# Attention decode with a side MLP on one core: K and V of a block through three rotating slots, each block finished before the next is scored

## The chip, the cores and the metric

The kernel runs on one core of one Trainium2 chip. The metric is the device time of one execution in microseconds, the median of the runs shown. Times inside the execution come from one profiled execution and count from the start of its span.

## What is computed

One token, `D = 1024`, goes through two branches that are added to it. Branch A is attention with 32 query heads on 4 key/value heads, over a cache of 65536 keys of 128 numbers. Branch B is a small MLP with two gelu stages. All tensors are bfloat16.

```python
xn = layernorm(x)
# A: 4 KV heads, 8 query heads on each, 65536 keys
q = xn @ wq                                   # 1024 x 4096
p = softmax((q . k_cache) * 128 ** -0.5)      # per head, over all keys
A = (p . v_cache) @ wo                        # 4096 x 1024
# B: h is shifted by quarters of its columns (S = 1: only zeros or the row itself)
h  = gelu(layernorm(xn) @ w1);  x1 = xn + shift(h) @ w2
B  = x1 + gelu(layernorm(x1) @ w3) @ w4       # 1024 x 3584, 3584 x 1024
out = x + A + B
```

With one row every shifted quarter is zero, so `x1` is `xn`. The kernel still reads `w1` and `w2`.

Nearly all the work is reading: 134.2 MB of cache (4 heads x 65536 keys x 128 x 2 bytes, for K and for V) and the rest weights, 169.87 MB in all.

## The kernel before, in words

**Blocks.** The cache of each KV head is cut into `NB = 2` blocks of 32768 keys. So there are `NU = 8` blocks `u`, and block `u` belongs to head group `g = u // 2`. K of a block, or V of a block, is one transfer of 128 partitions x 32768 bfloat16, 8.39 MB (`load`, L291 to L312). The weights come in similar pieces: `wq` and `wo` 8.39 MB each, `w3` 7.34 MB, `w12` (that is w1 and w2 in two transfers) 4.19 MB, `w4` 7.34 MB in five transfers.

**Slots.** SBUF holds three slots of that size (`slots`). `home` (L285 to L288) says which item lies where: K of even blocks in slot 0, K of odd blocks in slot 2, V of all blocks in slot 1 (the last V in slot 0). `wq`, `w3` and `w12` start in slots 0, 1 and 2, `wo` and `w4` end in 1 and 2.

**Recorded program.** The kernel does not issue its instructions at once. It records them in program order (`Program.add`); `plan` works out which semaphore each must wait for from the regions it reads and writes, and `emit` writes them out, each engine's in the recorded order. So the order of the calls in the source is the order on each engine, and an instruction that waits holds up all that stands behind it on its engine. Since all operations are emitted by the same helper lines, the profile shows few lines: L82 is every recorded DVE, ACT and POOL operation, L102 the weight loads, L106 the matmuls of `mm`, L116 `mm32`, L122 `turn32`, L89 the transfers. One reads it by tiles: `slot` (the three slots), `sc` (scores in PSUM), `p_sb` (the weights after the exponential), `oacc` (P·V in PSUM), `psB` (the final projection).

**Transfers.** All large loads stand on the queue of SP, in recorded order. A load into a slot waits until TensorE has read the last of what lay there.

**One block** passes through four steps:

- `scores(u)` (L453): DVE transposes K of the block in place, in 4 pieces (`slot<-slot`, 128x4096 as f32). After each piece TensorE runs 16 matmuls into `sc`, 64 in all. With the first block of a group POOL first places the queries in `qdiag`.
- `maxima(u)` (L469): a bound on the maximum: DVE reduces `sc` to `mx`, TensorE turns it, DVE reduces `m8` and scales it into `rep`, TensorE turns it back, DVE copies it to `nball`.
- `weights(u)` (L480): ACT takes the exponential of `sc` into `p_sb` and sums it, DVE transposes `p_sb`.
- `values(u, after)` (L486): 64 matmuls on V of the block into `oacc`; then the loads in `after` are recorded.

After the first block of a group ACT copies `oacc` to `og` (`first_rows`). After the second, `group_weights` and `group_rows` (DVE, one matmul) weigh and add the two and write the group's rows of `oT`, which is the left operand of `wo`.

**Order around the change** (L521 to L540). `compute_wq`, `compute_w3`, `compute_w12` come first, with the loads of K0 behind wq and of K1 and V0 behind w12. The main loop is software-pipelined by one block: the scores of block `u + 1` stand before the values of block `u`, and the loads of V `u + 1` and K `u + 3` come behind the values of `u`.

**The end.** DVE writes `o` into the free tail of w4's slot. 64 matmuls of `wo` add to `psB`, then 40 of `w4` (its first two transfers, 16 and 24 matmuls), DVE adds `o` (`og<-psB,slot`), and the last three transfers of `w4` go through narrow matmuls (20, 8 and 4 matmuls, the four of `pick` between the first two) into `pm`; ACT and DVE copy out, and one store writes the result. L-numbers of the listing are those of the profile.

Of the kernel before, what the change touches and what calls it, by code (L numbers as in the profile page):

```python
# [206 lines left out]
def kernel(  # L207
# [17 lines left out]
    HKV = A_k_cache.shape[1]  # L225
# [10 lines left out]
    NU = HKV * NB  # L236
# [7 lines left out]
    def sb(name, shape, dtype=F32):  # L244
        return nc.alloc_sbuf_tensor(name, list(shape), dtype)
# [4 lines left out]
    slots = [sb(f"slot{i}", [P, ROW], BF16) for i in range(3)]  # L250
# [31 lines left out]
        nb_pm[0] ^= 1  # L282
        return pm[nb_pm[0]]

    home = {"wq": 0, "w3": 1, "w12": 2, "wo": 1, "w4": 2, ("V", NU - 1): 0}  # L285
    for u in range(NU):
        home["K", u] = 0 if u % 2 == 0 else 2
        home.setdefault(("V", u), 1)  # L288
    tiles = {it: slots[i] for it, i in home.items()}

    def load(it):  # L291
        t = tiles[it]
        if it == "wq":
            prog.load("sp", t[:], A_wq.rearrange("(p c) n -> p (c n)", c=DC))
        elif it == "w3":
            prog.load("sp", t[:, 0:DC * F], B_w3.rearrange("(p c) f -> p (c f)", c=DC))
        elif it == "w12":
            prog.load("sp", t[:, 0:DC * D], B_w1.rearrange("(p c) n -> p (c n)", c=DC))
            prog.load("sp", t[:, DC * D:2 * DC * D], B_w2.rearrange("(m c) n -> m (c n)", c=DC))
        elif it == "wo":  # L300
            prog.load("sp", t[:], A_wo.rearrange("(p j) n -> p (j n)", p=P))
        elif it == "w4":
            w4_v = B_w4.rearrange("(m c) n -> m c n", c=FC)
            c0 = 0
            for n in W4_PIECES:
                prog.load("sp", t[:, c0 * D:(c0 + n) * D], w4_v[:, c0:c0 + n, :].rearrange("p c n -> p (c n)"))
                c0 += n
        else:
            kind, i = it
            g, b = divmod(i, NB)  # L310
            cache = A_k_cache if kind == "K" else A_v_cache
            prog.load("sp", t[:], cache[0, g, b * UKEYS:(b + 1) * UKEYS, :].rearrange("(p ct) d -> p (ct d)", p=P))  # L312

    load("wq")
    opening = len(prog.ops)
# [72 lines left out]
    def row_matmul(rep, cols, widths):  # L388
        for c in range(DC):
            for i, n in enumerate(widths):  # L390
                for q in range(4):
                    pe.mm(sc[32 * q:32 * q + 32, i, 0:n], rep[:, c, :], cols(c, i, q), c == 0, c == DC - 1,
                          (0, 32 * q), COLS)

    def compute_wq():
        wt = tiles["wq"][:].rearrange("p (c h a i) -> p c h a i", c=DC, a=4, i=32)
        row_matmul(xn_rep, lambda c, i, a: wt[:, c, 16 * i:16 * (i + 1), a, :], (512, 512))
        load(("K", 0))
        flat = p_sb[:, 0:1024]
        q_row = flat.rearrange("p (i n) -> p i n", i=2)  # L400
        dve.tensor_copy(out=q_row[:, 0, :], in_=sc[:, 0, :])
        act.copy(out=q_row[:, 1, :], in_=sc[:, 1, :])
        dve.transpose(out=flat, in_=flat)
        pq = next_pm()[:, 0:128].rearrange("p (x c) -> p x c", x=4)
        for x in range(4):
            pe.mm(pq[:, x, :], spread[:, x, :], flat[:, ::32], True, True)
        dve.tensor_copy(out=qx[:], in_=pq)
# [8 lines left out]
    def compute_w3():  # L416
        wt = tiles["w3"][:, 0:DC * F].rearrange("p (c m k) -> p c k m", c=DC, k=FC)
        row_matmul(xn2_rep, lambda c, i, a: wt[:, c, 16 * i:min(16 * (i + 1), FC), 32 * a:32 * (a + 1)],
                   (512, 32 * FC - 512))
        h_row = p_sb[:, 0:32 * FC]  # L420
        act.activation(out=h_row[:, 0:512], in_=sc[:, 0, :], func=ACTF.Gelu_apprx_tanh)
        act.activation(out=h_row[:, 512:], in_=sc[:, 1, 0:32 * FC - 512], func=ACTF.Gelu_apprx_tanh)
        dve.transpose(out=h_row, in_=h_row)
        dve.tensor_copy(out=hT[:], in_=h_row[:, ::32])

    def compute_w12():
        wt = tiles["w12"][:, 0:2 * DC * D].rearrange("p (w c n) -> p w c n", w=2, c=DC)
        for c in range(DC):
            for q in range(2):
                pe.mm(sc[0:32, q, :], xn2_rep[:, c, :], wt[:, 0, c, 512 * q:512 * (q + 1)], c == 0, c == DC - 1,  # L430
                      (0, 0), COLS)
        h1 = p_sb[0:32, 0:1024].rearrange("p (q n) -> p q n", q=2)
        act.activation(out=h1, in_=sc[0:32, 0:2, :], func=ACTF.Gelu_apprx_tanh)
        for c in range(DC):
            for j in range(2):
                row_acc(j, g_col[:], wt[:, 1, c, 512 * j:512 * (j + 1)], start=(c == 0))
        load(("K", 1))
        load(("V", 0))

    W = ROW // SETS  # L440

# [11 lines left out]
    def scores(u):  # L453
        g, b = divmod(u, NB)
        if b == 0:
            place_queries(g)
        t = tiles["K", u]
        cols = t[:].rearrange("p (s u k b x r) -> p s u k b x r", u=SUBS, s=SETS, k=16, b=2, r=2)
        for s in range(SETS):
            words = t[:, W * s:W * (s + 1)].bitcast(F32)  # L460
            dve.transpose(out=words, in_=words)
            for b2 in range(2):
                for r in range(2):
                    c0 = LEAD + P * (2 * b2 + r) - 8 * s
                    for e in range(SUBS):
                        pe.mm(sc[:, e, :], qdiag[:, c0:c0 + P], cols[:, s, e, :, b2, :, r],
                              s == 0 and b2 == 0 and r == 0, s == SETS - 1 and b2 == 1 and r == 1)

    def maxima(u):  # L469
        g, b = divmod(u, NB)  # L470
        dve.reduce_max(out=mx[:], in_=sc[:].rearrange("p e n -> p (e n)"), axis=AX.X)
        at = next_pm()
        pe.turn32(at[0:1, 0:P], mx[:, 0:1], ident_f[:])
        dve.tensor_reduce(out=m8[:], in_=at[0:1, 0:P].rearrange("o (j h) -> o h j", h=8), axis=AX.X, op=ALU.max)
        dve.tensor_scalar(out=rep[:].rearrange("o (j h) -> o j h", h=8),
                          in0=m8[:].unsqueeze(1).to_broadcast([1, P // 8, 8]), scalar1=-SCALE, scalar2=None, op0=ALU.mult)
        pe.turn32(at[:, P:P + 1], rep[0:1, :], ident_f[0:1, 0:1])
        dve.tensor_copy(out=nball[g % 2][:, b:b + 1], in_=at[:, P:P + 1])

    def weights(u):  # L480
        g, b = divmod(u, NB)
        act.activation(out=p_sb[:], in_=sc[:].rearrange("p e n -> p (e n)"), func=ACTF.Exp,
                       bias=nball[g % 2][:, b:b + 1], scale=SCALE, accum_out=lall[g % 2][:, b:b + 1])
        dve.transpose(out=p_sb[:], in_=p_sb[:])

    def values(u, after):  # L486
        vt = tiles["V", u][:].rearrange("p (s u t d) -> p s u t d", u=SUBS, s=SETS, t=16)
        for e in range(SUBS):
            for t in range(16):
                q = t % 4  # L490
                pe.mm(oacc[32 * q:32 * (q + 1), :], p_sb[:, 512 * e + 32 * t:512 * e + 32 * (t + 1)],
                      vt[:, :, e, t, :], e == 0 and t < 4, e == SUBS - 1 and t >= 12, (0, 32 * q), COLS)
        for it in after:
            load(it)

    def first_rows():
        act.copy(out=og[:], in_=oacc[:])

    def group_weights(g):
        dve.tensor_reduce(out=negmg[:], in_=nball[g % 2][:], axis=AX.X, op=ALU.min)  # L500
        act.activation(out=wb[:], in_=nball[g % 2][:], func=ACTF.Exp, bias=negmg[:, 0:1], scale=-1.0)
        dve.tensor_scalar(out=og[:], in0=og[:], scalar1=wb[:, 0:1], scalar2=None, op0=ALU.mult)
        dve.tensor_tensor_reduce(out=lw[:], in0=lall[g % 2][:], in1=wb[:], scale=1.0, scalar=0.0,
                                 op0=ALU.mult, op1=ALU.add, accum_out=ol[:, DH:DH + 1])
# [16 lines left out]
    compute_wq()  # L521
    compute_w3()
    compute_w12()
    stream = [[("V", u + 1), ("K", u + 3)] for u in range(NU - 3)] + [[("V", NU - 2), ("V", NU - 1)], ["wo", "w4"]]
    scores(0)
    load(("K", 2))
    maxima(0)
    weights(0)
    for u in range(NU - 1):
        g, b = divmod(u, NB)  # L530
        scores(u + 1)
        maxima(u + 1)
        if b == 1:
            group_weights(g)
        values(u, stream[u])
        if b == 0:
            first_rows()
        else:
            group_rows(g)
        weights(u + 1)  # L540
    group_weights(HKV - 1)
    values(NU - 1, [])
    group_rows(HKV - 1)

    o = tiles["w4"][0:64, FC * D:FC * D + D].bitcast(F32)
    dve.tensor_scalar(out=o, in0=x_halves[:], scalar1=ln_s1[0:64, 0:1], scalar2=ln_s2[0:64, 0:1],
# [75 lines left out]
```

## Time and profile before

| what | value |
| --- | --- |
| median of 3 runs | 405.64 us (403.96 to 405.98) |
| the profiled execution, own time | 404.04 us |
| its span, first to last instruction | 402.6 us |
| mean granted TensorE clock | 0.792 |
| TensorE matmuls busy | 221.1 us (55%) |
| DVE busy | 209.9 us (52%) |
| ACT busy | 27.2 us (7%) |
| read from memory | 169.87 MB, 422 GB/s over the span |

The page has six parts: busy time of each engine; the span in 40 slices of about 10 us, each digit a busy share in tenths; the DMA queues; the chain of work that ended last; the costliest groups of instructions with the idle time ahead of them and what ended it; and the DMA issues. Behind the page the trace answers finer questions: the instructions in order of time, and the busy time of each engine and the DMA share in any stretch. In the rows of the timeline the first two numbers are start and busy time in us; the bracket at the end says how long the engine stood idle and what released it. SPq is SP's queue at the moment it issues a transfer.

### The profile page before, as it was taken

How to read it: one execution, taken by the hardware profiler on the slowest of the kernel's cores; microseconds unless marked ns; L12 is line 12 of the kernel's file. 1: busy time of each engine (PE TensorE's matmuls, PEld its weight loads, DVE VectorE, ACT ScalarE, POOL GpSimd, SP SyncE). 2: the span in 40 equal slices, each digit the busy share in tenths (PEclk: the TensorE clock that was granted, in tenths of full speed). 3: DMA queues.
4: the chain of work that ended last, by engine and by line, in shares of the span. 5: the costliest groups of instructions: out<-in, count | busy, mean ns of one | idle time of the engine just before them, and what ended most of it. 6: DMA issues, size and time to landing. Idle time of an engine off the chain costs nothing.

```text
span 402.6 us, 2557 instructions
## 1 busy us (share of the span) xinstructions
PE 221.1 (55%) x1360; PEld 46.2 (11%) x890; DVE 209.9 (52%) x156; ACT 27.2 (7%) x35; POOL 6.2 (2%) x29
## 2 busy tenths in 40 slices
PE   0250970591794497369607850976096329625096
PEld 0210010000001012101200020002011101112043
DVE  0520010966963983696249647950795669322101
ACT  1010030002002000200020020002000200020000
POOL 2000000000000000000000000000000000000000
PEclk9996896696699597659667985696589859987579
DMA  9989999999997999999999999999999999999995
GB/s 365 462 371 430 457 417 449 463 430 423 423 417 314 417 469 464 417 417 417 425 417 443 482 412 417 423 430 417 488 425 417 423 430 423 484 423 418 394 440 242
DMA packets 3760, 170.03 MB, mean 422 GB/s; under 512 B 419, under 2 KB 421, under 8 KB 678
## 3 DMA queue, kind: packets, MB, share of 16 engines
q1 hardware_dynamic: 3744, 169.87, 98.1%
q8 instruction: 9, 0.15, 0.1%
q14 instruction: 1, 0.01, 0.0%
q10 hardware_dynamic: 6, 0.00, 0.0%
HBM read 169.87 MB, written 0.00 MB: 422 GB/s over the span
## 4 chain that ended last, share of the span: by engine, by line
DMA 49%; PE 25%; DVE 23%; ACT 1%; SPq 1%; issue 1%
DMA slot<-in_A_k_cache_dram 33%; PE sc L106 16%; DVE slot L82 16%; DMA slot<-in_B_w_dram 11%; PE oacc L106 7%; DMA slot<-in_A_wq_dram 5%; DVE mx L82 3%; DVE p_sb L82 2%; ACT p_sb L82 1%; PE pm L122 1%; SPq L89 1%; DVE m L82 0%; DVE og L82 0%; DVE rep L82 0%; DVE ol L82 0%
## 5 line engine op out<-in xcount | busy, mean ns | idle before, releaser
L106 PE MATMUL sc<-slot,qdiag 128*128 128x512 bf16 x512 | 130.7, 417 | 91.2 <-DVE slot L82 91.0
L82 DVE STREAM_TRANSPOSE slot<-slot 128x4096 f32<-128x4096 f32 x32 | 139.2, 4408 | 27.1 <-DMA slot<-in_A_k_cache_dram 27.1
L82 DVE STREAM_TRANSPOSE p_sb<-p_sb 128x2048 bf16<-128x2048 bf16 (+2 forms) x10 | 20.8, 2083 | 55.9 <-ACT p_sb L82 55.7
L106 PE MATMUL oacc<-slot,p_sb 128*32 128x512 bf16 x512 | 42.5, 506 | 8.9 <-DMA slot<-in_A_v_cache_dram 8.9
L102 PEld LDWEIGHTS <-qdiag 128*128 128x128 bf16 x128 | 13.3, 104 | 204.1 <-issue 204.1
L82 DVE TENSOR_REDUCE mx<-sc 128x1 f32<-128x2048 f32 x8 | 18.3, 2292 | 30.1 <-PE sc L106 30.1
L106 PE MATMUL sc<-slot,ln_rep_b 128*32 128x512 bf16 (+1 forms) x80 | 16.3, 834 | 9.7 <-DMA slot<-in_B_w_dram 9.5
L102 PEld LDWEIGHTS <-p_sb 128*32 128x32 bf16 x512 | 16.6, 123 | 31.5 <-issue 20.6
L82 ACT ACTIVATE p_sb<-sc,nball 128x2048 bf16<-128x2048 f32 x8 | 15.8, 1970 | 49.6 <-DVE nball L82 36.0
L106 PE MATMUL psB<-slot,oT 128*32 128x512 bf16 x64 | 9.3, 461 | 11.0 <-DMA slot<-in_A_wo_dram 11.0
L82 DVE SCALAR_TENSOR_TENSOR og<-oacc,wb,og 128x512 f32<-128x512 f32 x4 | 3.0, 751 | 20.1 <-PE oacc L106 20.1
L82 DVE TENSOR_TENSOR og<-psB,slot 64x512 f32<-64x512 f32 x1 | 0.7, 684 | 24.2 <-PE psB L106 24.2
L122 PE MATMUL pm<-ident_f,mx 128*1 128x128 f32 x8 | 2.4, 295 | 19.1 <-DVE mx L82 19.1
L82 ACT COPY og<-oacc 128x512 f32<-128x512 f32 x4 | 2.3, 586 | 142.8 <-PE oacc L106 142.8
L116 PE MATMUL pm<-ol,selx 128*128 128x129 f32 x8 | 2.6, 414 | 10.6 <-DVE ol L82 10.6
L116 PE MATMUL pm<-ln_rowsum_a,msk 128*128 128x1 f32 x2 | 0.6, 363 | 13.4 <-DVE ln_rowsum_a L82 13.4
L106 PE MATMUL sc<-slot,ln_rep_a 128*32 128x512 bf16 x64 | 5.1, 488 | 4.7 <-DMA slot<-in_A_wq_dram 4.7
L82 POOL COPY qdiag<-qx 32x32 bf16<-32x32 bf16 x16 | 3.2, 203 | 261.5 <-PE sc L106 235.4
L82 ACT ACTIVATE wb<-nball,negmg 128x2 f32<-128x2 f32 x4 | 1.2, 296 | 89.6 <-DVE negmg L82 89.6
L82 DVE STREAM_TRANSPOSE p_sb<-x_row 32x256 bf16<-32x256 bf16 x4 | 2.5, 616 | 7.5 <-DMA x_row<-in_A_x_dram 7.5
L102 PEld LDWEIGHTS <-oT 128*32 128x32 bf16 x64 | 4.2, 113 | 15.7 <-issue 12.3
L106 PE MATMUL psB<-slot,hT 128*32 128x512 bf16 x40 | 4.7, 379 | 1.2 <-DMA slot<-in_B_w_dram 1.2
(86 smaller groups left out, 61.2 us busy)
## 6 DMA issues: line engine op xcount, KB each, us to landing
slot<-in_B_w_dram SPq DMA_DIRECT2D x1, 7168.0 KB, 37.7
slot<-in_B_w_dram SPq DMA_DIRECT2D x3, 2048.0 KB, 43.2
slot<-in_B_w_dram SPq DMA_DIRECT2D x1, 3072.0 KB, 39.5
slot<-in_B_w_dram SPq DMA_DIRECT2D x1, 1280.0 KB, 42.1
slot<-in_B_w_dram SPq DMA_DIRECT2D x1, 512.0 KB, 42.9
slot<-in_B_w_dram SPq DMA_DIRECT2D x1, 256.0 KB, 43.0
slot<-in_A_k_cache_dram SPq DMA_DIRECT2D x8, 43.6
slot<-in_A_v_cache_dram SPq DMA_DIRECT2D x8, 27.8
```

The lines of the kernel that those rows point to most:

```text
L82: return program.add(Op(engine, lambda: method(*args, **kw), reads, writes, alone=kw.get("accum_out") is not None))
L89: return self.add(Op(engine, lambda: e.dma_start(out=out, in_=in_), [], [out], transfer=True))
L102: self.add(Op("pe", lambda: pe.ldweights(lhsT, tile_position=pos), [lhsT], []))
L106: return pe.add_instruction(mybir.InstMatmult(name=nc.get_next_instruction_name(), engine=mybir.EngineType.PE, start_tensor_calc=start, st ...
L116: return self.add(Op("pe", lambda: pe.matmul(out, lhsT=lhsT, rhs=rhs, start=start, stop=stop, tile_position=pos, skip_group_check=True), [ ...
L122: return self.add(Op("pe", lambda: pe.transpose(out, in_, identity), [in_, identity], [out]))
```

## The change

The items are put in one list in the order of their use, `wq, w3, w12, K0, V0, K1, V1, ..., K7, V7, wo, w4`, and item `i` lies in slot `i % 3`. As soon as the last matmul that reads item `i` is recorded, the load of item `i + 3` is recorded (`freed`). K and V thus alternate in the stream, where before K1 came ahead of V0 and each K ran one block further ahead. `freed` is also called behind w3's matmuls. The main loop is no longer shifted: scores, maxima, weights and values of one block, then the next block.

```diff
-    home = {"wq": 0, "w3": 1, "w12": 2, "wo": 1, "w4": 2, ("V", NU - 1): 0}
-    for u in range(NU):
-        home["K", u] = 0 if u % 2 == 0 else 2
-        home.setdefault(("V", u), 1)
-    tiles = {it: slots[i] for it, i in home.items()}
+    stream = ["wq", "w3", "w12"] + [(kind, u) for u in range(NU) for kind in "KV"] + ["wo", "w4"]
+    tiles = {it: slots[i % 3] for i, it in enumerate(stream)}
...
+    def freed(it):
+
+        n = stream.index(it) + 3
+        if n < len(stream):
+            load(stream[n])
...
     def compute_wq():
...
-        load(("K", 0))
+        freed("wq")
...
     def compute_w3():
...
+        freed("w3")
         h_row = p_sb[:, 0:32 * FC]
...
     def compute_w12():
...
-        load(("K", 1))
-        load(("V", 0))
+        freed("w12")
...
     def scores(u):
...
+        freed(("K", u))
...
-    def values(u, after):
+    def values(u):
...
-        for it in after:
-            load(it)
+        freed(("V", u))
...
-    stream = [[("V", u + 1), ("K", u + 3)] for u in range(NU - 3)] + [[("V", NU - 2), ("V", NU - 1)], ["wo", "w4"]]
-    scores(0)
-    load(("K", 2))
-    maxima(0)
-    weights(0)
-    for u in range(NU - 1):
+    for u in range(NU):
         g, b = divmod(u, NB)
-        scores(u + 1)
-        maxima(u + 1)
+        scores(u)
+        maxima(u)
+        weights(u)
         if b == 1:
             group_weights(g)
-        values(u, stream[u])
+        values(u)
         if b == 0:
             first_rows()
         else:
             group_rows(g)
-        weights(u + 1)
-    group_weights(HKV - 1)
-    values(NU - 1, [])
-    group_rows(HKV - 1)
```

## The prediction

> **What bounds the kernel now.** I read the page's slices first, then the queues, then the rows in which an engine wakes on a K or V transfer, and last a fine table of the DMA share around the one dip.
>
> ```profile
> DMA  9989999999997999999999999999999999999995
> GB/s 365 462 371 430 457 417 449 463 430 423 423 417 314 417 469 464 417 417 417 425 417 443 482 412 417 423 430 417 488 425 417 423 430 423 484 423 418 394 440 242
> ...
> q1 hardware_dynamic: 3744, 169.87, 98.1%
> ```
>
> SP's queue keeps the 16 DMA engines busy for 98.1% of the span, while TensorE and DVE are busy 55% and 52%. The stream of loads is the bound. Inside it one slice stands out: the thirteenth (121 to 131 us), digit 7, 314 GB/s. The page's chain of waits names DVE and TensorE for nearly half of the span; it follows who released each load, and a load that is released long before its turn in the queue costs nothing, so I go by the DMA row.
>
> The stream's own speed is in the rows that wake on it:
>
> ```profile
> 70.00 17.42 DVE L82 STREAM_TRANSPOSE slot<-slot 128x4096 f32<-128x4096 f32 x4 [15.58 <-DMA slot<-in_A_k_cache_dram]
> 208.92 4.45 DVE L82 STREAM_TRANSPOSE slot<-slot 128x4096 f32<-128x4096 f32 x1 [3.02 <-DMA slot<-in_A_k_cache_dram]
> 325.33 4.45 DVE L82 STREAM_TRANSPOSE slot<-slot 128x4096 f32<-128x4096 f32 x1 [4.00 <-DMA slot<-in_A_k_cache_dram]
> 364.04 5.28 PE L106 MATMUL oacc<-slot,p_sb 128*32 128x512 bf16 x64 [8.87 <-DMA slot<-in_A_v_cache_dram]
> 383.40 9.28 PE L106 MATMUL psB<-slot,oT 128*32 128x512 bf16 x64 [10.96 <-DMA slot<-in_A_wo_dram]
> ```
>
> These are K0, K4, K7, V7 and wo landing. K7 to V7 is two loads (V6, V7) in 38.71 us, V7 to wo one in 19.36: **19.355 us for a load of 8.39 MB**, 433 GB/s. K0 to K4 is seven loads in the old order (K1, V0, K2, V1, K3, V2, K4): 7 x 19.355 = 135.5 us, but they took 138.92. So 3.4 us are lost there; K4 to K7 loses another 0.3 (six loads, 116.41 against 116.13). Where:
>
> ```profile
> 122.00:124.00 2.00, 0.74 (x10) 0.43 (x14) 1.23 (x4) 0.00 (x0) 0.00 (x0) 1.00 1.06 459
> 124.00:126.00 2.00, 2.00 (x44) 0.96 (x39) 0.00 (x0) 0.00 (x0) 0.00 (x0) 1.00 0.31 131
> 126.00:128.00 2.00, 1.31 (x28) 0.52 (x17) 0.00 (x0) 0.64 (x2) 0.00 (x0) 1.00 0.04 8
> 128.00:130.00 2.00, 0.00 (x0) 0.00 (x0) 0.06 (x1) 1.91 (x2) 0.00 (x0) 1.00 1.55 524
> 130.00:132.00 2.00, 0.00 (x0) 0.00 (x0) 2.00 (x1) 0.00 (x0) 0.00 (x0) 0.97 1.13 492
> 132.00:134.00 2.00, 0.00 (x0) 0.00 (x0) 2.00 (x2) 0.00 (x0) 0.00 (x0) 0.50 0.68 295
> ...
> 91.13 0.33 SPq L89 DMA_DIRECT2D slot<-in_A_k_cache_dram  x1
> 127.36 0.33 SPq L89 DMA_DIRECT2D slot<-in_A_v_cache_dram  x1
> ```
>
> The last two columns are DMA share and GB/s. The queue runs dry from about 125 to 128.5: K2, issued at 91.13, is all that is left, and V1 is issued only at 127.36, when values(0) has freed V's only slot, because scores(1) stood ahead of values(0). The six windows moved 2 x (459+131+8+524+492+295) = 3,818 KB; at 433 GB/s 12 us hold 5,200. The missing 1,380 KB are 3.2 us; the same sum from 120 to 134 gives 2.9. I take **3.0 us** for the gap. The other 0.7 of the lost 3.7 (3.4 + 0.3) has no cause that I can see.
>
> **The change, part by part.** *Work:* no instruction of TensorE, DVE, ACT or POOL is added or dropped; the 18 K, V and wo, wq loads, w3, w12 and w4 stay the same transfers, so 169.87 MB and SP's 0.33 to 0.45 us of issue each. Some SP rows gain a wait on TensorE. Cost of these edits: nothing while the queue holds another load, as below.
>
> *The stream, first load by load.* Up to K0 (70.00) nothing changes: wq, w3, w12, K0 in the old order. From there each load takes 19.355 as long as the next is issued before the present one's packets run out; the dip shows that 127.36 was about 2 to 2.5 us too late for a stream that dried at 125, 3 us ahead of K2's landing (70.00 + 3 x 19.355 = 128.07). So a lead of over 3 us ahead of the predecessor's landing is needed. The leads:
>
> - V0 after w3's matmuls, about 52 us (40.00 + 12.95 in the timeline, one w12 matmul in it); ahead of it K0 lands at 70.0: lead 18. K1 at 58.2 as now.
> - V1 after scores(0), 91.1 as K2 is now; K1 lands at 108.7: lead 17.6.
> - K2 after values(0). Its row: p_sb is transposed at 99.26 (96.95 + 2.31), that is K0 + 29.26; values took 3.64 to 6.56 us in the eight blocks, so 103 to 106, with V1 to land at 128.1: lead 22.
> - Each later block repeats this at K's landing + 21.1 and + 36.
>
> No lead comes near 3 us. SP is one queue, and these releases come in the order of the queue, so none holds up another. So the dip goes and no new one comes: **-3.0 us**. Bounds: if all that the stream lost goes, -3.7; if it is lost at another place, 0. I take 3.0, since the windows show these bytes missing at this release.
>
> *The block's chain, now serial.* K to transposed p_sb 29.26; values 5.3 to 6.6 behind 8 us of idle TensorE (the 64 that ran behind 8.87 us of idle took 5.28, others up to 6.56); on the second block of a group the DVE rows to oT, 369.37 to 373.64, 4.3 us. DVE is held 29.3 us in even blocks (the next transposes don't wait for values) and 29.3 + 6.6 + 4.4 = 40.3 in odd ones: 69.6 us in two blocks, against 4 x 19.355 = 77.4 of transfers. It fits; an odd block makes the next K start up to 1.6 us after it lands, and the even block takes that back. Hidden, by 7.8 us in two blocks.
>
> *The end.* This is what is late next. K7 moves from two loads ahead of V7 to one: it lands at 341.0 (70.00 + 14 x 19.355), 15.6 us later than now, and wo at 379.7, two loads after K7. From K7: 29.3 + 5.3 to 6.6 + 4.3 = 38.9 to 40.2 us to oT, against 38.71 to wo. So wo's matmuls start 0.2 to 1.5 us after wo has landed; now they start on it. Is there slack behind them?
>
> ```profile
> 395.61 2.77 PE L106 MATMUL psB<-slot,hT 128*32 128x512 bf16 x24 [1.20 <-DMA slot<-in_B_w_dram]
> 398.70 0.73 PE L106 MATMUL pm<-slot,hT 128*32 128x256 bf16 x20 [0.33 <-DMA slot<-in_B_w_dram]
> 400.57 0.29 PE L106 MATMUL pm<-slot,hT 128*32 128x256 bf16 x4 [0.22 <-DMA slot<-in_B_w_dram]
> ```
>
> TensorE waits 1.20 us for w4's second transfer and 0.33 and 0.22 for the third and fifth: about 1.6 us in all, since the DVE sum and the matmul on it overlap part of the 0.33. Late by 0.2 to 1.5, the end is still set by the last transfer. Cost 0, bounds 0 to +1.1 (wo's 9.28 us may have 1.2 us more at half clock: 1.5 + 1.2 - 1.6).
>
> One rule of the skill speaks against the change here. The Trainium skill, TensorE: Matmul & The Clock Gate, Part 1, says that an array idle for a window of about 3.4 us falls to half clock and needs about 3.4 us of work to come back. By it every values(u) would now start at half clock and take about 5.3 us (30 matmuls cold, 34 warm; an estimate), wo would start 0.2 us late and the end would not move; by the row of 6.56 us the return can take longer, 1.5 late, and the end stays too, but with 0.1 us to spare. Another, DMA: Bandwidth & Descriptors, Specifications, gives about 358 GB/s as the limit of one core's memory reads; the rows here show 433. By 358 the 1,380 KB would be worth 3.9 us (an estimate) in place of 3.2; the measured rate decides.
>
> **Sum.** 404.04 (span 402.6 and 1.44 around it) - 3.0 + 0 = **401.0 us**. The profiled execution lies near the lowest of the runs, 1.6 under their median of 405.64. That fits one thing in the rows: values(0), which issues V1, took its shortest time here (3.64 us; six of the other seven blocks took 5.28 to 6.56), and 1.6 to 2.9 us more would lengthen the dip by as much. If so, the longer runs lose it with the change, and the time after does not depend on it; this is argued, not shown. So I keep 401.0 also against the median.
>
> **Rivals.**
>
> - *The end comes late* (wo's start more than 1.6 us behind its transfer, clock still half): 401.0 + 1 to 2 = 402 to 403 us. For it: the slack is thin. Against: it takes the longest values and a longer cold start together.
> - *The lost time moves, no change*: the 3.0 us come back as a rate below 433 GB/s when K and V alternate, or as a dry spot at a release I take for early. 404 us. For it: 0.7 us of loss has no cause here. Against: V, K, V, K already alternate from V1 to K7 in the stream, at 19.4 a load.
> - *Slower: the tail runs at half clock throughout.* K7 now lands 15.6 us later, so all behind it is exposed. Values 2 x 3.64 = 7.3, rows 4.4, wo's 64 at 0.23 us (twice the 2.77/24 of the w4 row) 14.8, w4's 40 9.2, the rest about 3.4: 341.7 (K7, with the 0.7) + 29.3 + 39.1 = 410.1 for the last matmul against 400.86 now, so 413 us. It decides from the point where the tail is over 1.6 + 3.0 = 4.6 us late. Against: in all rows TensorE comes back to full clock while it works.
>
> **Numbers.** Forecast 0.72, late end 0.14, no change 0.09, slower 0.05. Likeliest 401.0. Low end: all 3.7 us gone, 400.3, and 0.3 for the reading of the rows: 400.0. High end: the late end's middle and the 2.0 us by which the runs of before spread meet at 403.0. The rest, under 0.2, lies outside. A measurement here tells 0.5% (2 us) from no change: faster by more than that 0.86, within it 0.09, slower 0.05.
>
> **What would show it.** Right: no dip in the DMA row; V1 issued near 91; DVE wakes on K1 near 108.7, on K7 at 341 to 342, every K 38.7 apart; wo's first matmul released by oT, not by its transfer, at most 1.5 us after 380; a wait for w4's last transfer near 397. Wrong: K rows over 39 us apart, a new dip, oT later than 383, or the last matmuls with no wait on a transfer.

## The result and the profile after

The changed kernel takes **400.70 us** (median of 4 runs, 400.63 to 400.92); the kernel before took 405.54 beside it (4 runs, 403.96 to 405.98). The ratio is 0.9888, 95% interval 0.9862 to 0.9915. The forecast was 401.0. The profiled execution took 400.65 us, its span is 399.2. The two profiled executions thus differ by 3.39 us (404.04 against 400.65), the medians by 4.84.

The slices of the changed kernel's page:

```profile
DMA  8989999999999999999999999999999999999996
GB/s 342 486 381 419 468 422 420 428 453 473 422 420 427 427 415 433 447 473 420 415 427 427 427 433 447 461 420 420 427 429 433 433 447 448 420 420 427 404 442 254
```

The thirteenth slice, 7 and 314 GB/s before, is 9 and 427 now. Of the other slices only the first reads lower, 8 for 9; it lies in the opening, and K0 landed no later for it: the first of the 16 DMA engines finished K0 at 68.29 us in both kernels. Now the rows of the timeline that answer to those shown of before: DVE waking on K0, K1 and K7, SP issuing V1 and K2, and TensorE in the tail.

```profile
70.41 17.42 DVE L82 STREAM_TRANSPOSE slot<-slot 128x4096 f32<-128x4096 f32 x4 [16.39 <-DMA slot<-in_A_k_cache_dram]
109.10 17.42 DVE L82 STREAM_TRANSPOSE slot<-slot 128x4096 f32<-128x4096 f32 x4 [9.28 <-DMA slot<-in_A_k_cache_dram]
341.31 17.42 DVE L82 STREAM_TRANSPOSE slot<-slot 128x4096 f32<-128x4096 f32 x4 [7.92 <-DMA slot<-in_A_k_cache_dram]
...
91.58 0.33 SPq L89 DMA_DIRECT2D slot<-in_A_v_cache_dram  x1
105.64 0.33 SPq L89 DMA_DIRECT2D slot<-in_A_k_cache_dram  x1
...
380.17 8.77 PE L106 MATMUL psB<-slot,oT 128*32 128x512 bf16 x64 [1.25 <-DVE oT L82]
392.23 2.77 PE L106 MATMUL psB<-slot,hT 128*32 128x512 bf16 x24 [1.57 <-DMA slot<-in_B_w_dram]
395.32 0.73 PE L106 MATMUL pm<-slot,hT 128*32 128x256 bf16 x20 [0.32 <-DMA slot<-in_B_w_dram]
397.17 0.29 PE L106 MATMUL pm<-slot,hT 128*32 128x256 bf16 x4 [0.22 <-DMA slot<-in_B_w_dram]
```

K0 to K7 is 14 loads in 270.90 us (341.31 - 70.41), 19.35 each: nothing is lost any more. V1 leaves at 91.58, not at 127.36. wo's matmuls are now released by `oT`, no longer by wo, and w4's last transfer still sets the end, at 397.17 (400.57 before).

### The profile page after: what moved, and what is told of

Its sections match the earlier page's. It is cut to its first block, busy times and chain, and to the rows that moved or that the text cites. A ratio compares the mean times of both kernels' runs of the same rounds, so it can differ in the third digit from the quotient of the medians.

```text
span 399.2 us, 2557 instructions
## 1 busy us (share of the span) xinstructions
PE 222.5 (56%) x1360; PEld 45.2 (11%) x890; DVE 210.3 (53%) x156; ACT 27.6 (7%) x35; POOL 6.2 (2%) x29
## 4 chain that ended last, share of the span: by engine, by line
DMA 56%; DVE 21%; PE 17%; another core or an unknown queue 2%; ACT 2%; issue 0%; SPq 0%
DMA slot<-in_A_k_cache_dram 42%; DVE slot L82 15%; PE sc L106 12%; DMA slot<-in_B_w_dram 9%; DMA slot<-in_A_wq_dram 5%; PE oacc L106 4%; DVE p_sb L82 2%; DVE mx L82 2%; ACT p_sb L82 2%; PE pm L122 1%; DVE m L82 0%; DVE rep L82 0%; DVE nball L82 0%; DVE x_halves L82 0%
## 5 line engine op out<-in xcount | busy, mean ns | idle before, releaser
L106 PE MATMUL sc<-slot,qdiag 128*128 128x512 bf16 x512 | 129.2, 413 | 67.3 <-DVE slot L82 67.1
L106 PE MATMUL oacc<-slot,p_sb 128*32 128x512 bf16 x512 | 46.0, 538 | 37.5 <-DVE p_sb L82 18.8
L122 PE MATMUL pm<-ident_f,rep 1*128 1x1 f32 x8 | 1.8, 230 | 5.0 <-DVE rep L82 5.0
L102 PEld LDWEIGHTS <-ln_rep_b 128*32 128x32 bf16 x40 | 1.9, 112 | 23.3 <-issue 23.1
```

The source lines that it names most:

```text
L102: self.add(Op("pe", lambda: pe.ldweights(lhsT, tile_position=pos), [lhsT], []))
L106: return pe.add_instruction(mybir.InstMatmult(name=nc.get_next_instruction_name(), engine=mybir.EngineType.PE, start_tensor_calc=start, st ...
L122: return self.add(Op("pe", lambda: pe.transpose(out, in_, identity), [in_, identity], [out]))
```

## The experiments

The theory: the stream of loads is the bound; a load costs time only if it is released too shortly ahead of the landing of the one before it, and what the shifted loop did was to release each V one block's scores late. Rivals: the rotation of the slots, with K and V in turn, is what feeds the queue; a single bad release that any local mend would cure; an end set by the chain behind K7.

**The serial loop on the old slots** (loads in the old order, K1 ahead of V0).

```diff
...
-    for u in range(NU - 1):
+    for u in range(NU):
...
-        scores(u + 1)
-        maxima(u + 1)
+        scores(u)
+        if u + 2 < NU:
+            load(("K", u + 2))
+        if u == NU - 1:
+            load("w4")
+        maxima(u)
+        weights(u)
...
-        values(u, stream[u])
...
+        if u == NU - 2:
+            load(("V", NU - 1))
+        values(u, after)
...
```

`after` is V `u + 1` for the first six blocks and `wo` for the seventh.

> The loop of the changed kernel (scores, maxima, weights, values of one block, then the next) with the slots and the load order of before (K1 ahead of V0, all V in slot 1). Theory (what counts is how long ahead of the landing of its predecessor a load is released): V1 is issued near 114 us (V0 lands at 108.7, values 5.5), 14 us ahead of K2's landing at 128, so no dip; but values(6) waits for V6 (344.6) and scores(7) stands behind it on TensorE, so the rows of the last group come near 383, 3 us behind the landing of wo, past the 1.6 us of slack: 401 to 403 us. Rival (the rotation of the slots, K and V in turn, is what feeds the queue): the dip stays, 404 to 406 us.

400.83 us (4 runs, 400.69 to 400.99) against 406.46 of before in the same job; ratio 0.9861 (0.9831 to 0.9891). The slices of its page, and V1's issue:

```profile
DMA  8989999999999999999999999999999999999996
...
114.33 0.33 SPq L89 DMA_DIRECT2D slot<-in_A_v_cache_dram  x1
```

There is no dip. So **the order of the loop alone gives the whole gain**, and the rotation is not needed for it. My worry about its end was wrong: the rows of the last group came at 380.9, not 383. V6 landed at 341.4 and not 344.6, as the whole stream was some 3 us earlier, and TensorE caught up with scores(7).

**One block mended, the rest shifted.**

```diff
+    values(0, stream[0][:1])
+    first_rows()
+    scores(1)
+    load(stream[0][1])
+    maxima(1)
+    weights(1)
-    for u in range(NU - 1):
+    for u in range(1, NU - 1):
```

> The kernel before with one edit: values(0) and the load of V1 ahead of scores(1), the rest still shifted by one block. Theory: the dip at V1's release goes (issue near 114), but values(1) still stands behind scores(2), so V2 is issued at 165 to 168 with K3 landing at 166.8: the queue runs dry there instead, 402 to 405 us. Rival (one bad release, and all is well once it is mended): 400.7 to 401.2 us, no dip.

405.19 us (10 runs, 403.79 to 405.57); ratio 0.9976 (0.9952 to 1.0). The slices of its page, and SP's queue:

```profile
DMA  8989999999999999799999999999999999999995
...
113.72 0.33 SPq L89 DMA_DIRECT2D slot<-in_A_v_cache_dram  x1
...
166.84 0.33 SPq L89 DMA_DIRECT2D slot<-in_A_v_cache_dram  x1
```

V1 leaves in time, at 113.72. The 7 has moved to the seventeenth slice: V2 leaves at 166.84, and K3 lands at 167.15. A local mend only hands the dip to the next release.

**The rotation with the shifted loop.** The changed kernel with this loop:

```diff
-    for u in range(NU):
+    scores(0)
+    maxima(0)
+    weights(0)
+    for u in range(NU - 1):
...
-        scores(u)
-        maxima(u)
-        weights(u)
+        scores(u + 1)
+        maxima(u + 1)
...
+        weights(u + 1)
+    group_weights(HKV - 1)
+    values(NU - 1)
+    group_rows(HKV - 1)
```

> The rotating slots and load order of the changed kernel with the shifted loop of before (scores of block u+1 ahead of values of block u). Theory: with three slots in turn the loads V2, K2 wait for scores(1) and values(0), and from then on each K is issued only after the block before it has been used; the queue is dry some 20 us in each block: K rows about 60 us apart, 540 to 600 us. Rival (the rotation by itself feeds the queue): about 401 us.

560.21 us, one run. Its slices and two K wakes:

```profile
DMA  9999999997991189705992099803993099819950
...
172.72 17.43 DVE L82 STREAM_TRANSPOSE slot<-slot 128x4096 f32<-128x4096 f32 x4 [27.57 <-DMA slot<-in_A_k_cache_dram]
236.43 17.42 DVE L82 STREAM_TRANSPOSE slot<-slot 128x4096 f32<-128x4096 f32 x4 [27.48 <-DMA slot<-in_A_k_cache_dram]
```

K rows 63.7 us apart instead of 38.7, and the queue stands still in every block. Rotation is no gain by itself: it needs the serial loop.

**The kernel before, again.**

> The kernel before once more, unchanged. Theory: the dip is as long as values(0) makes it: V1 is issued at 123.7 us plus the time of values(0) (3.6 to 6.6 us), and K4 lands at 208.9 plus what that is over 3.64 us; with 5.3 us or more the time is near 405.6. Rival (the spread of the runs of before comes from the rate of the transfers): K4 later or earlier with V1's issue at 127.4, or loads of 19.6 us and more far from the dip.

406.76 us, one run. The rows of values(0) and of V1's issue, and K4's wake:

```profile
124.10 6.32 PE L106 MATMUL oacc<-slot,p_sb 128*32 128x512 bf16 x64
130.47 0.33 SPq L89 DMA_DIRECT2D slot<-in_A_v_cache_dram  x1
...
211.75 17.42 DVE L82 STREAM_TRANSPOSE slot<-slot 128x4096 f32<-128x4096 f32 x4 [4.02 <-DMA slot<-in_A_k_cache_dram]
```

The same program, with values(0) in 6.32 us instead of 3.64: V1 3.1 us later, K4 2.8 later, the time 2.7 longer. That is where the spread of before (403.5 to 407.6 over 13 runs in this job) can come from, shown in two executions; in the changed kernel what waits for values(0) is K2, issued 22.8 us ahead of the landing before it, and its four runs lie within 0.3 us.

**V1 released a little late, in the changed kernel.** The hold makes the load wait for a region that values(0) writes.

```diff
+    held_by = {}
...
+            op = prog.load("sp", t[:], cache[0, g, b * UKEYS:(b + 1) * UKEYS, :].rearrange("(p ct) d -> p (ct d)", p=P))
+            if it in held_by:
+                op.reads.append(region(held_by[it]))
...
-        freed(("K", u))
+        if u != 0:
+            freed(("K", u))
...
+        if u == 0:
+            held_by[("V", 1)] = oacc[:]
+            freed(("K", u))
         freed(("V", u))
```

> The changed kernel with one release moved: V1 is issued behind values(0), with K2, and not behind scores(0). Theory, sharpened by the three dips seen so far (lead of the release ahead of the predecessor's landing 0.67, 0.31 and -2.14 us; loss 3.0, 3.6 and 5.9): loss = 3.7 us less the lead. V1 would be issued at 105.6, K1 lands at 109.1: lead 3.4, loss 0.3, 400.7 to 401.2 us, later K rows 0.3 later than in the changed kernel. Rival (the loss is set by the landing itself: no loss as long as the release comes ahead of it by the 2 us from issue to first byte, and none here; or a loss at any lead under 6 us, the smallest lead without loss in the kernel before): 400.7 with no shift at all, or 402 to 404.

401.71 us (4 runs, 401.66 to 402.25), 1.0 more than the changed kernel and above the 400.7 to 401.2 expected. V1 left at 105.43, 3.5 us ahead of K1. At the spot the stream lost 0.3 us, as expected; over all the loads up to wo it lost 0.85. So the size was off, by what the loads behind the late one lost. The rival's 2 us from issue to first byte are not what the trace has either: where the queue had run dry, the first packet began 1.0 us behind the issue. The page's DMA row has no digit below 8: a loss of 0.85 us is below what a slice shows.

**V1 released much too late, in the changed kernel.**

```diff
             dve.transpose(out=words, in_=words)
+            if u == 1 and s == 0:
+                held_by[("V", 1)] = t[:, 0:W]
+                load(("V", 1))
+                load(("K", 2))
...
```

The hold is the one of the run before, and the loads of V1 and K2 are taken out of their places behind scores(0) and values(0).

> The changed kernel with V1's release held until DVE has transposed the first piece of K1, so that the queue must run dry: V1 is issued near 113.6 us, K1 lands at 109.1, lead -4.5. Theory: loss 3.7 + 4.5 = 8.2 us in the stream, and all of it in the end: 408.5 to 409.5 us; from the dip on loads of 19.35 to 19.4 us. Rival (the stream makes good what it lost, since no slot waits for compute later): under 404.

408.96 us, one run. Two windows of its dip (the last two columns are DMA share and GB/s), V1's issue, and the tail:

```profile
104.00:106.00 2.00, 1.15 (x24) 0.41 (x17) 0.00 (x0) 0.59 (x1) 0.00 (x0) 1.00 1.25 532
106.00:108.00 2.00, 0.00 (x0) 0.00 (x0) 0.00 (x0) 0.00 (x0) 0.00 (x0) 1.00 0.00 0
...
113.59 0.33 SPq L89 DMA_DIRECT2D slot<-in_A_v_cache_dram  x1
...
405.49 0.29 PE L106 MATMUL pm<-slot,hT 128*32 128x256 bf16 x4 [0.22 <-DMA slot<-in_B_w_dram]
```

A window counts a packet where it begins: the last ones of K1 begin by 105.98 and end between 106.9 and 108.7, engine by engine, and K1 lands at 109.1. V1's first packet begins at 114.55, 1.0 us behind the issue at 113.59. All of it stays lost: the last transfer is 8.3 us later than in the changed kernel (405.49 against 397.17).

The five kernels with one late release in one table. The lead is from the issue to the landing of the load before it on all 16 DMA engines; the loss is read from the trace's landing records, on the fastest of the engines, at the late load and from K0 to wo (16 loads; 309.6 us in the changed kernel).

| kernel | lead, us | lost at the late load | lost up to wo | lead + lost up to wo, us |
| --- | --- | --- | --- | --- |
| V1 a little late | 3.54 | 0.32 | 0.85 | 4.4 |
| before | 0.67 | 3.00 | 3.56 | 4.2 |
| first block mended | 0.31 | 3.58 | 3.76 | 4.1 |
| before, again | -2.14 | 5.94 | 6.38 | 4.2 |
| V1 much too late | -4.50 | 8.23 | 8.57 | 4.1 |

Over 8 us of lead the loss is 4.1 to 4.4 us less the lead: about 3.8 at the spot and 0.2 to 0.6 later.

The trace's records also show what the 3.8 at the spot is made of. In these five runs the late load lands on the fastest engine 21.1 to 21.3 us after its issue, 1.8 to 2.0 more than the 19.35 of a load in the stream. The rest is how far the slowest engine lagged behind the fastest on the load before, 1.6 to 2.0 us, because the lead is taken to the slowest one's landing. The rotation with the shifted loop bears this out far below: V3, with a lead of -21.16 us behind a load with a lag of 1.85, lost 24.92 (sum 3.8); V7, with -21.30 behind a lag of 0.59, lost 23.78 (sum 2.5).

In the changed kernel the smallest lead is 16.0 us (V7 issued at 325.29, K7 landing at 341.3); in the serial loop on the old slots it is 7.0 (K4 at 179.62, V2 at 186.6), and that loses nothing either. Leads between 3.5 and 7.0 were not tried one by one. The runs hold three by chance: V3 with the first block mended (4.66 us) took 19.39 us, so it lost at most 0.04; V2 in the kernel before (6.43) took 19.62 and wo in the rotation with the shifted loop (4.55) 19.65, but both came soon after a dry spell, where loads are slower anyway.

**The tail: oT later by one or two transposes.**

```diff
+            if u == NU - 1:
+                for _ in range(1):
+                    dve.transpose(out=p_sb[:], in_=p_sb[:])
             group_rows(g)
```

> The changed kernel with one more DVE transpose of p_sb (2.31 us; of no use, behind values(7), whose p_sb is no longer read) ahead of the last group's rows: oT comes 2.3 us later. Theory (slack of the tail: the waits 1.57 + 0.32 + 0.22 for the transfers of w4, of which some 1.6 to 2.0 us can be used): the end 0.3 to 0.8 us later, 401.0 to 401.5 us; the wait for w4's second transfer gone. Rival 1 (the chain behind K7 already sets the end): 2.3 us later, 403.0. Rival 2 (more slack than that): no change, 400.7.

402.44 us (4 runs, 401.80 to 402.79): more than expected. Here wo's and w4's matmuls in its profiled execution, of 401.80 us, the shortest of the four:

```profile
382.75 9.68 PE L106 MATMUL psB<-slot,oT 128*32 128x512 bf16 x64 [1.25 <-DVE oT L82]
392.26 4.05 PE L106 MATMUL psB<-slot,hT 128*32 128x512 bf16 x36
...
398.10 0.51 PE L106 MATMUL pm<-slot,hT 128*32 128x256 bf16 x12
```

No wait for a transfer is left. wo starts 2.58 us later than in the changed kernel (382.75 against 380.17), but its 64 matmuls also take 9.68 instead of 8.77. The windows say why; behind TensorE's busy time stand its granted clock, the DMA share and GB/s. First the changed kernel, then this one:

```profile
380.00:384.00 4.00, 3.83 (x20) 0.58 1.04 444
384.00:388.00 4.00, 4.00 (x40) 1.00 1.00 430
```

```profile
380.00:384.00 4.00, 1.82 (x8) 0.65 1.01 432
384.00:388.00 4.00, 4.00 (x22) 0.50 1.03 442
```

At 384 to 388 TensorE has its full clock in the one and half of it in the other: 40 matmuls against 22. So the lateness came to 2.58 + 0.91 = 3.5 us, and the end moved by 1.15: the slack was 2.3 us.

With two transposes:

> The same with two more transposes: oT 4.6 us later. Theory: the end 2.6 to 3.1 us later, 403.3 to 403.8 us, no wait of TensorE for any transfer of w4. Rival 1 (the chain already sets the end): 405.3. Rival 2 (slack of over 4 us): 400.7.

403.96 us, one run. wo started at 385.90, 5.7 us later (values(7) took 0.67 us more, too), took 8.60, and the end came 3.2 us later, just above the 2.6 to 3.1 expected: 5.73 - 0.17 - 3.23 = 2.3 us of slack again. The slack is real and the chain behind K7 does not set the end of the changed kernel; what I had left out of these two expectations was the clock.

## Why the prediction was right, step by step

- **The bound, and the dip as its only large loss: right.** Taking the dip away moved the end by 3.4 us, about what was missing there, and putting a dip back cost what it measured.
- **The gain of 3.0 us: right in kind, a little small.** The profiled executions differ by 3.39 us. On the fastest DMA engine K0 to wo took 313.2 us before and 309.6 after: 3.56 us gone, 3.00 of them at V1, as forecast, and 0.56 in the loads behind it. So the 0.7 "with no cause that I can see" went too. In every run of the table the stream loses 0.2 to 0.6 us more in the loads behind the late one, in the runs with no late release nothing; so it belongs to the dry spell. Why is open: the packets of all 16 engines take longer for some us at several places behind it. By the wakes (400.57 - 70.00 against 397.17 - 70.41) the stream gained 3.8 us, but a wake waits for the slowest engine: the 0.4 us by which K0's wake is later after the change are that engine's lag (2.09 us against 1.69), since the fastest lands K0 at 68.29 in both.
- **The lead a load needs: "over 3 us", measured 4.1 to 4.4, or 3.7 to 3.9 at the late load itself.** The step took the drying of the queue from windows of 2 us (see below). With leads of 16 us and more it did not matter.
- **Leads in the serial order: right.** V1 91.1 forecast, 91.58 measured; K2 103 to 106, 105.64; K1 108.7, 109.1; K7 341.0, 341.3.
- **The serial chain fits under the transfers: right.** K6, behind an odd block, was begun at 304.16 with no wait, 1.6 us after its landing in the records; K7 waited 7.92 us on its transfer.
- **The tail: right, on a clock that happened to be no worse.** wo's matmuls began 0.2 us behind its landing (forecast 0.2 to 1.5), and wo took 8.77 us, less than the 9.28 of before. The slack was 2.3 us, not 1.6.
- **The clock rule** (the Trainium skill, TensorE: Matmul & The Clock Gate, Part 1: half clock after an idle window of about 3.4 us, and about 3.4 us of work to come back). The eight values took 5.00 to 6.53 us here, none the 3.64 that two blocks had before (the other six took 5.28 to 6.56). In the trace's record the granted clock is one half when each of the eight starts, behind 4.7 us of idle, and full again 2.8 to 5.9 us later; the two of 3.64 had full clock all through. This agrees with the page on the loss of clock; on its return, the estimate of 5.3 was met by the shorter ones and passed by the longer, by up to 1.2 us. In the tail with one more transpose half clock lasted for 5.3 us of work (382.75 to 388.04).
- **The memory limit** (the Trainium skill, DMA: Bandwidth & Descriptors, Specifications: about 358 GB/s for one core): a load of 8.39 MB every 19.35 us, 433 GB/s, over 14 loads on end shows no such limit for this core.
- **The median of before: right, as far as two profiles show it.** The profiled execution was one of its shorter ones, with values(0) at 3.64 us, as argued; the second profile of it, with 6.32, showed the other case. So the medians moved further than the forecast 3.0.

## What to carry to other kernels

Where one queue of loads is the bound, look at each load's release against the landing of the load ahead of it, not at what the engines wait for: in this kernel a lead of 7 us was free, and below some 4 us each us less cost a us, about half of the 4 for starting a dry queue and half because one DMA engine lags behind the others. Shifting compute ahead to keep the engines busy gained nothing here, and because it held a buffer longer it took time from the stream. Before an order is made serial, check what then follows the last load: here 2.3 us of slack was all that kept the chain behind K7 off the end.

## What the runs showed of the hardware

Windows shorter than a packet's time mislead. A packet of 64 KB takes 2.42 us here, a window counts all of its time and bytes where it begins, and most of the 16 engines run nearly in step; so a window of 2 us swings with no idle time behind it. The changed kernel, which never runs dry:

```profile
122.00:124.00 2.00, 2.00 (x11) 0.19 (x2) 2.00 (x2) 0.00 (x0) 0.00 (x0) 1.00 1.21 524
124.00:126.00 2.00, 2.00 (x11) 0.28 (x3) 2.00 (x1) 0.00 (x0) 0.00 (x0) 1.00 0.46 197
```

The prediction read 0.31 at 124 to 126 as the start of the dip; most of that was this. By the packets themselves the engines of before ran dry one after the other between 125.8 and 127.6 and began again from 128.3. The sum over 12 us and the wakes of K and V were sound; single windows were not.

The other: of the 16 DMA engines the slowest lands each load 2.1 us behind the fastest in the changed kernel, from w1 on (0.5 us at w3), and no later load closes the gap. The last transfer pays it once. Why it opens was not looked into.
